# Query and key rows placed by head, so that one SBUF-to-SBUF transfer per block replaces the trip through DRAM

## The chip, the cores and the metric

The kernel runs on one NeuronCore of a Trainium2 chip. The metric is the device time of one launch in microseconds (us). Before the change three timed runs gave 1001.59 us in the median (996.12, 1001.59 and 1002.09); the execution that the profiler recorded took 993.12 us.

## What is computed

Two layers follow each other. The first is a linear attention with a complex decay, for 4 sequences of 768 steps with 8 heads of width 48:

```
mag = sqrt(a_re^2 + a_im^2);  a = (a_re, a_im) * min(mag, 0.999) / (mag + 1e-6)
for t in range(768):                       # for every batch and head
    S_re, S_im = a_re*S_re - a_im*S_im + outer(k[t], v[t]),  a_re*S_im + a_im*S_re
    y[t] = q[t] @ S_re                     # S: 48 x 48
```

The second is a mixture of four experts on the 3072 rows y (8 heads * 48 = 384 wide), with `p = domain_probs / (sum + 1e-9)`:

```
out = sum_e p[:, e] * (relu(x @ w1[e]) @ w2[e])      # w1: 384 x 1024, w2: 1024 x 384
```

All is float32. The matrix products of the experts are made from operands split into a high and a low part (names ending in h and l, three products for one).

## The kernel before, in words

**Groups.** The 3072 time steps are cut into 12 groups of 256 (g = 0 to 11), each of two chunks of 128 (c = 0, 1). A group's attention needs no step loop: with the running product A of the decays, the scores between q*A and k/A within a chunk are a matrix product, and a state Gs of [48 real + 48 imaginary rows, 8 heads, 48] carries what came before.

**Stage one** (0 to about 616 us) works as a pipeline. While TensorE runs the first two experts on group g-1 (`moe1`: eight steps, each of a first-layer part, tile `ph`, line 235, and a second-layer part, `po`, line 256), VectorE and ScalarE prepare group g (`norm`, `prefix`, `finish`: `head` makes Q, line 504, `tail` makes K, line 527). The attention of g is placed between the steps of group g-1 by `between`: from step `FIRST[g]` on (6, 5, 5, 4, 4 for groups 2 to 6, then 3) one piece of `attention` is issued per step. `advance` deals out the preparation by a budget of microseconds per step (`STEP`, `MORE`); `yield None` in `front` is a hold that lasts until the attention of g-1 has been issued. The framework then orders each engine's instructions by a simulated timeline, within the order that `behind` and `keep_in_program_order` fix; on the chip each engine runs its list in order.

**Rows.** Q and K are made with 128 of the 384 rows (head, component) on the partitions, in three columns j: row h*48+d lies at partition (h*48+d) mod 128. Heads 2 and 5 straddle two columns. The scores want each head's 48 components on partitions 0 to 47 (real) and 64 to 111 (imaginary): tiles `Qst` and `Kst`. For groups 2 to 11 `trip` (line 532) brings them there through DRAM: two transfers (real, imaginary) `q_d<-Q` or `k_d<-K` out (line 536) and two `Qst<-q_d` or `Kst<-k_d` back (line 543), all on SyncE's queue (SP). For groups 0 and 1 K goes by two TensorE transposes (lines 576 and 585, with ScalarE copies at 577 and 586) and Q by `pick` (matmuls with parts of the identity, group 0, chunk 0) or by `trip`.

**Attention of one group.** Before: the pieces are `turn0` (K of chunk 0 transposed into `KT`), scores of chunk 1 then chunk 0 (`sc`, line 619; VectorE multiplies them by a mask into `scs`, line 630); then `turn1`; then the values (`yp`, lines 650 and 660) of chunk 0 with the state increment of chunk 0 (`dp`, line 595; VectorE adds it to the state, line 605) inside them, behind the first pair of heads; then increment and values of chunk 1. The PSUM tiles of all of these share four buffers (tag "pa"). At the end `store_y` sends y to DRAM, `load_x` fetches it back as `xa`, and the next `moe1` starts on it.

**Behind it.** The loads of group g+1's inputs (`load_qk`, line 356, and `load_a`, line 349) wait until K of g has landed (`last["q"]`). `late_weights` (lines 780 to 802) runs beside the last groups: it loads weights (`lw`, line 784), sums and splits them on VectorE and ScalarE, and writes them to DRAM. **Stage two** (about 616 us to the end) runs the other two experts, lines 972 to 984, and touches nothing of the above.

Of the kernel before, what the change touches and what calls it, by code (L numbers as in the profile page):

```python
# [8 lines left out]
F32 = mybir.dt.float32  # L9
F32R = mybir.dt.float32r  # L10
AF = mybir.ActivationFunctionType
# [4 lines left out]
B, H, S, D = 4, 8, 768, 48  # L16
HD = H * D
# [43 lines left out]
STEP = {1: 4.2, 2: 4.2, 3: 4.2, 4: 4.2, 5: 4.2}  # L61
MORE = (1.5, 2.3, 0.5)
HOFF = 96
WIDE = 32 + P + 48
DMA_SCRATCH = 4096
XOF = (0, 1, 2, 3, 4, 5, 6, 7, 0, 8, 9, 6, 10, 11, 12, 13, 14, 15, 5, 9)
# [55 lines left out]
def fast_path(ctx, tc, qkP, aP, vP, probsP, w, out, flag):  # L122
# [164 lines left out]
    with ExitStack() as c1:  # L287
# [166 lines left out]
        def pick(g, nm, X, dst, s, w):  # L454
            n = 4 if w == C else 3
            for h0 in range(0, H, n):
                hs = range(h0, min(h0 + n, H))
                ps = ps_a.tile([M, len(hs), w], F32, tag="pa", name=f"{nm}p{g}_{s}_{h0}")
                for h in hs:
                    js = [j for j in range(NJ) if -D < h * D - j * P < P]  # L460
                    for j in js:
                        o = 32 + h * D - j * P
                        for c in range(2):
                            ins = nc.tensor.matmul(ps[c * IM:(IM, M)[c], h - h0, :], wide[:, o:o + (IM, D)[c]],
                                             X[:, c, j * CG + s, :w], start=(j == js[0]), stop=(j == js[-1]))
                nc.scalar.activation(dst[:, h0:h0 + len(hs), s, :w], ps, AF.Copy)
            return ins

# [60 lines left out]

            return Q, K, head, tail  # L530

        def trip(nm, X, dst, lo=0, hi=CG, prev=None):
            w = X.shape[-1] if hi == CG else C
            dt = dram.tile([2, HD, hi - lo, w], F32, name=nm)
            for c in range(2):
                sent = nc.sync.dma_start(dt[c].rearrange("(j p) n t -> p j n t", p=P),
                                         X[:, c].rearrange("p (j n) t -> p j n t", n=CG)[:, :, lo:hi, :w])
                if prev is not None:
                    behind(sent, prev)

            def back(prev=None):
                for c in range(2):
                    landed = nc.sync.dma_start(dst[c * IM:c * IM + D, :, lo:hi, :w],
                                               dt[c].rearrange("(h d) n t -> d h n t", d=D))
                    if prev is not None:
                        behind(landed, prev)
                return landed
            back.sent = sent
            return back

        def t_factors(g):
            Tr, Ti = Qst[0:D, :, CG - 1, C:], Qst[IM:M, :, CG - 1, C:]
# [9 lines left out]
        def chunk(g, c, K, y):  # L562
# [7 lines left out]
            def turned():  # L570
                if last and g >= NSEL:
                    return
                for i in range(2):
                    kt_ps = ps_a.tile([P, HD], F32, tag="pa", name=f"ktp{g}_{c}_{i}")
                    for j in range(NJ):
                        ins = nc.tensor.transpose(kt_ps[:, j * P:(j + 1) * P], K[0][:, i, j * CG + c, :], ident)
                    state["kt", g, c] = nc.scalar.activation(KT[:, c, :, i * IM:i * IM + D],
                                                             kt_ps.rearrange("p (h d) -> p h d", d=D), AF.Copy)
                return ins

            def turned_back():
# [57 lines left out]
                            behind(ins, prev)  # L639
                    nc.vector.tensor_tensor(scs[2 * c + hf], s_ps, near_mask.unsqueeze(1).broadcast_to([P, 4, C]), op=ALU.mult)  # L640

            def values(joined=False, after=None):
                y_ps = ps_a.tile([P, HP, C], F32, tag="pa", name=f"yp{g}_{c}")
                for p in reversed(range(HP)):
                    ws = (IM, D) if g < XSEL else (D, D)
                    pair = [(h * D, ws[u], y_ps[u * IM:u * IM + ws[u], p, :]) for u, h in enumerate((2 * p, 2 * p + 1))]
                    for o, n, yo in pair:
                        h = o // D
                        vo = o if h < HP else o + HD // 2
                        ins = nc.tensor.matmul(yo, vc[:, vo:vo + n], scs[2 * c + h // 4][:, h % 4, :],  # L650
                                               start=True, stop=first)
                        if joined:
                            tc.keep_in_program_order(ins)
                        if after is not None and p == HP - 1 and o == h * D and not h & 1:
                            behind(ins, wts["w1e"])
                        joined = True
                    if not first:
                        for o, n, yo in pair:
                            st = state[g, c].rearrange("m h d -> m (h d)")
                            ins = nc.tensor.matmul(yo, st[:, o:o + n], Qc[:, o // D, :], start=False, stop=True)  # L660
                            tc.keep_in_program_order(ins)
                    if after is not None and p == HP - 1:
                        after()
                state["yl", g, c] = ins
                for us in ((slice(0, M),) if g < XSEL else (slice(0, D), slice(IM, M))):
                    state["y", g, c] = nc.scalar.activation(y[us, :, cs], y_ps[us], AF.Copy)
# [30 lines left out]
        def near_attention(g, QK):  # L697
            Q, K = QK
            y = small.tile([M, HP, G], F32, tag="y", name=f"y{g}", bufs=1)
            (turn0, back0, inc0, sc0, val0), (turn1, back1, inc1, sc1, val1) = (chunk(g, c, K, y) for c in range(CG))  # L700
            if g == 0:
                state["pq"] = pick(g, "q", Q, Qst, 0, C)
                yield
            else:
                yield trip(f"q_d{g}_0", Q, Qst, 0, 1)()
                yield trip(f"q_d{g}_1", Q, Qst, 1)()
            state["tk"] = turn0()
            state["bk"] = back0()
            inc0()
            sc0((0,))  # L710
            if g > 0:
                sc0((1,))
            yield
            if g == 0:
                yield trip(f"q_d{g}", Q, Qst, 1)()
# [12 lines left out]
            rotate(g)  # L728
# [6 lines left out]
        def attention(g, QK):  # L735
# [2 lines left out]
            turn0()  # L738
            sc1()
            sc0(joined=True)  # L740
            yield turn1()
            val0(True, after=lambda: inc0(True))
            inc1(True)
            val1(True)
            t_factors(g)
# [71 lines left out]
        def front(g, A, qk):  # L817
# [34 lines left out]
            yield 3.9  # L852
            last["act"] = head(0, CG)
            yield 3.0
            qb = trip(f"q_d{g}", Q, Qst)
            yield None
            last["dve"] = tail(0, CG)
            yield 4.8
            kb = trip(f"k_d{g}", K[0], Kst)
            qb()  # L860
            last["q"] = kb()
            todo[g] = attention(g, (Q, K))

        x = {}
# [651 lines left out]
```

## Time and profile before

| What | Value |
|---|---|
| timed runs, median (lowest, highest) | 1001.59 us (996.12, 1002.09) |
| the profiled execution | 993.12 us, of which the span of instructions is 991.4 us |
| TensorE matmul busy | 936.7 us, 94% of the span |
| VectorE busy | 745.9 us, 75% |
| ScalarE busy | 479.4 us, 48% |
| GpSimd busy | 166.5 us, 17% |
| mean granted TensorE clock | 0.986 of full speed |
| DMA | 141.89 MB, HBM read 92.13 MB and written 48.43 MB |

Read the shares with the stages in mind: VectorE's 75% is 38 to 39 us in each cycle of some 41 to 48 us in stage one, and less in stage two. TensorE's full clock (1.0) is 2.4 GHz, 0.5 is 1.2 GHz.

### The profile page before, as it was taken

The numbers are of one execution on the slowest core, as the hardware profiler recorded it, in microseconds if no ns is written. First come the engines' busy times: TensorE is split into PE (matmuls) and PEld (weight loads), VectorE is DVE, ScalarE is ACT, GpSimd is POOL, SyncE is SP. The second block draws the span as 40 slices with busy tenths as digits, with TensorE's granted clock in tenths as the row PEclk, the third lists the DMA queues.
The fourth block names the chain that finished last, engine by engine and source line by source line (L and its number), as shares of the span: only waits on it lengthen the run. The fifth ranks groups of instructions, "written<-read, shape, count | busy, mean of one in ns | idle before, by whom it ended". The sixth has DMA issues, their size and how long they took to land.

```text
span 991.4 us, 18889 instructions
## 1 busy us (share of the span) xinstructions
PE 936.7 (94%) x7365; PEld 913.2 (92%) x7365; DVE 745.9 (75%) x1630; ACT 479.4 (48%) x954; POOL 166.5 (17%) x207
## 2 busy tenths in 40 slices
PE   5799989899999989989998999999999999999997
PEld 3699988898999989989998999999999999999997
DVE  7789979788989989969896583767676748576643
ACT  6756435263644727354453354645454546454430
POOL 6020000000000000000000005533433342323000
PEclk9899989999999999999999999999999999999999
DMA  9495274655748567484939769431513443231112
GB/s 317 121 200 154 64 193 109 169 132 154 170 149 189 155 146 185 107 198 129 222 110 262 274 191 305 101 97 48 129 48 116 158 137 101 66 97 48 49 48 75
DMA packets 99154, 141.89 MB, mean 143 GB/s; under 512 B 7360, under 2 KB 79728, under 8 KB 99056
## 3 DMA queue, kind: packets, MB, share of 16 engines
q1 hardware_dynamic: 87856, 113.80, 39.9%
q0 software_dynamic: 11200, 26.79, 11.6%
q8 instruction: 60, 0.98, 0.4%
q14 instruction: 38, 0.31, 0.1%
HBM read 92.13 MB, written 48.43 MB: 142 GB/s over the span
## 4 chain that ended last, share of the span: by engine, by line
PE 65%; DVE 13%; DMA 12%; ACT 6%; issue 2%; SPq 1%; DVEq 0%; ACTq 0%
PE pob L972 19%; PE pb L972 16%; PE ph L235 11%; PE po L256 10%; DMA Kst<-k_d 3%; PE sc L619 3%; DMA k_d<-K 2%; DMA q_d<-Q 1%; DMA lw<-w 1%; DMA wst<-w 1%; PE dp L595 1%; DVE scs L630 1%; PE yp L650 1%; PE yp L660 1%; DMA xa<-y_d 1%
## 5 line engine op out<-in xcount | busy, mean ns | idle before, releaser
L972 PE MATMUL pob<-shi,hid 128*128 128x384 f32 x528 | 148.6, 335 | 0.5 <-DVE hid L981 0.5
L256 PE MATMUL po<-whi,hh 128*128 128x384 f32 x384 | 131.6, 343 | 8.5 <-ACT acc L755 6.0
L256 PE MATMUL po<-wlo,hh 128*128 128x384 f32 x384 | 130.1, 339 | 0.0
L246 ACT ACTIVATE hh<-ph 128x512 fp32r<-128x512 f32 x96 | 56.8, 593 | 113.5 <-PE ph L235 113.0
L984 POOL TENSOR_TENSOR Z<-Z 128x384 f32<-128x384 f32 x84 | 89.7, 1088 | 109.1 <-DVE xl L978 46.2
L235 PE MATMUL ph<-xha,whi 128*128 128x256 f32 x576 | 103.3, 286 | 3.9 <-ACT xha L222 3.9
L235 PE MATMUL ph<-xla,whi 128*128 128x256 f32 x576 | 102.0, 285 | 1.3 <-DVE xla L224 1.3
L235 PE MATMUL ph<-xha,wlo 128*128 128x256 f32 x576 | 101.7, 283 | 0.0
L972 PE MATMUL pb<-xh,shi 128*128 128x384 f32 x291 | 97.2, 335 | 1.2 <-DVE pb L978 1.2
L972 PEld LDWEIGHTS pob<-shi,hid 128*128 128x128 f32 x528 | 96.5, 188 | 1.2 <-DVE hid L981 1.1
L972 PE MATMUL pb<-xl,shi 128*128 128x384 f32 x288 | 96.2, 334 | 0.0
L972 PE MATMUL pb<-xh,slo 128*128 128x384 f32 x288 | 96.2, 334 | 0.0
L235 PEld LDWEIGHTS ph<-xha,whi 128*128 128x128 f32 x576 | 86.7, 191 | 6.3 <-ACT xha L222 4.7
L972 PE MATMUL pob<-slo,hid 128*128 128x384 f32 x264 | 88.2, 334 | 0.0
L247 DVE SCALAR_TENSOR_TENSOR hl<-ph,hh 128x512 fp32r<-128x512 f32 x96 | 65.9, 687 | 28.9 <-ACT hh L246 28.1
L256 PE MATMUL po<-whi,hl 128*128 128x384 f32 x384 | 85.2, 339 | 1.6 <-DVE hl L247 1.5
L235 PEld LDWEIGHTS ph<-xla,whi 128*128 128x128 f32 x576 | 83.3, 191 | 2.3 <-DVE xla L224 1.5
L235 PEld LDWEIGHTS ph<-xha,wlo 128*128 128x128 f32 x576 | 83.0, 190 | 0.7 <-issue 0.7
L256 PEld LDWEIGHTS po<-whi,hh 128*128 128x128 f32 x384 | 73.2, 191 | 9.5 <-ACT acc L755 6.4
L975 ACT ACTIVATE SN<-pb 128x384 f32<-128x384 f32 x96 | 47.3, 492 | 67.0 <-PE pb L972 59.7
L978 DVE TENSOR_TENSOR xl<-Z,xh 128x384 fp32r<-128x384 f32 x104 | 60.1, 607 | 21.6 <-ACT xh L975 13.8
L256 PEld LDWEIGHTS po<-wlo,hh 128*128 128x128 f32 x384 | 73.3, 191 | 0.0
(233 smaller groups left out, 2039.7 us busy)
## 6 DMA issues: line engine op xcount, KB each, us to landing
qk<-qkP SPq DMA_DIRECT2D x24, 384.0 KB, 4.0
acc_d<-acc POOLq DMA_DIRECT2D x24, 384.0 KB, 4.9
ACC<-acc_d SPq DMA_DIRECT2D x48, 192.0 KB, 2.9
A<-aP SPq DMA_DIRECT2D x22, 384.0 KB, 5.8
q_d<-Q SPq DMA_DIRECT2D x20, 387.0 KB, 4.0
Qst<-q_d SPq DMA_DIRECT2D x20, 387.0 KB, 5.1
k_d<-K SPq DMA_DIRECT2D x20, 384.0 KB, 4.3
Kst<-k_d SPq DMA_DIRECT2D x20, 384.0 KB, 6.0
```

What stands on the lines that cost most here:

```text
L235: ins = nc.tensor.matmul(ph[:, u, :], wt[:, j * P:(j + 1) * P], xt[:, j, :], start=(n == 0), stop=(n == 3 * NJ - 1))
L246: wts["hh"] = nc.scalar.activation(hh, ph, AF.Relu)
L247: nc.vector.scalar_tensor_tensor(hl, ph, 0.0, hh, op0=ALU.max, op1=ALU.subtract)
L256: nc.tensor.matmul(po[t], part[0][:, u, t * P:(t + 1) * P], wts[i][n][:, HD:], start=(i % FE == 0 and part[0] is hh and n == 0), stop=(i % ...
L595: ins = nc.tensor.matmul(d_ps[o:o + n, h, :], KT[:, c, h, o:o + n], vc[:, h * D:(h + 1) * D], start=True, stop=True)
L619: ins = nc.tensor.matmul(to, k, q, start=True, stop=True)
L630: nc.vector.tensor_tensor(to, x, m.broadcast_to([m.shape[0], 4] + list(m.shape[2:])), op=ALU.mult)
L650: ins = nc.tensor.matmul(yo, vc[:, vo:vo + n], scs[2 * c + h // 4][:, h % 4, :], start=True, stop=first)
L972: return tc.keep_in_program_order(nc.tensor.matmul(*args, **kw))
L975: return pin(nc.scalar.activation(dst, src, fn, scale=scale))
L978: pin(nc.vector.tensor_tensor(dst, x, y, op=op))
L984: nc.gpsimd.tensor_tensor(dst, x, y, op=op)
```

## The change

The host lays the 384 rows out in another order, given by `ROWS` (first partition, count, columns, first component, first head): blocks of partitions, each of which holds for every column j one head's (or part of one head's) consecutive components. Partitions 0 to 47 hold heads 0, 1, 2 (columns 0, 1, 2), partitions 48 to 95 heads 3, 4, 5; the last 32 partitions hold heads 6 and 7: components 0 to 31 in columns 0 and 1, components 32 to 47 of both in column 2. With that each block goes from Q or K straight to its place in `Qst` or `Kst` by one transfer, `send`: five blocks times real and imaginary, ten transfers for Q and ten for K. `pick` and the copy of the transposed K (`turned`) follow the new order; the latter takes three ScalarE copies for one. The send of Q stands behind the hold and ahead of `tail`. In `attention` the first increment `inc0` moves from inside the values of chunk 0 to right behind the scores of chunk 0.

```diff
+ROWS = ((0, 48, (0, 1, 2), 0, 0), (48, 48, (0, 1, 2), 0, 3), (96, 32, (0, 1), 0, 6), (96, 16, (2,), 32, 6),
+        (112, 16, (2,), 32, 7))
...
-        def trip(nm, X, dst, lo=0, hi=CG, prev=None):
+        def send(X, dst, lo=0, hi=CG, prev=None):
             w = X.shape[-1] if hi == CG else C
-            dt = dram.tile([2, HD, hi - lo, w], F32, name=nm)
             for c in range(2):
-                sent = nc.sync.dma_start(dt[c].rearrange("(j p) n t -> p j n t", p=P),
-                                         X[:, c].rearrange("p (j n) t -> p j n t", n=CG)[:, :, lo:hi, :w])
-                if prev is not None:
-                    behind(sent, prev)
-            def back(prev=None):
-                for c in range(2):
-                    landed = nc.sync.dma_start(dst[c * IM:c * IM + D, :, lo:hi, :w],
-                                               dt[c].rearrange("(h d) n t -> d h n t", d=D))
+                src = X[:, c].rearrange("p (j n) t -> p j n t", n=CG)[:, :, lo:hi, :w]
+                for p, n, j, d, h in ROWS:
+                    landed = nc.sync.dma_start(dst[c * IM + d:c * IM + d + n, h:h + len(j), lo:hi, :w],
+                                               src[p:p + n, j[0]:j[-1] + 1])
                     if prev is not None:
                         behind(landed, prev)
-                return landed
-            back.sent = sent
-            return back
+            return landed
...
-                    state["kt", g, c] = nc.scalar.activation(KT[:, c, :, i * IM:i * IM + D],
-                                                             kt_ps.rearrange("p (h d) -> p h d", d=D), AF.Copy)
+                    kj, to = kt_ps.rearrange("t (j p) -> t j p", j=NJ), KT[:, c, :, i * IM:i * IM + D]
+                    nc.scalar.activation(to[:, :6].rearrange("t (a j) d -> t a j d", j=NJ),
+                                         kj[:, :, :2 * D].rearrange("t j (a d) -> t a j d", d=D), AF.Copy)
+                    nc.scalar.activation(to[:, 6:, :32], kj[:, :2, 2 * D:], AF.Copy)
+                    state["kt", g, c] = nc.scalar.activation(
+                        to[:, 6:, 32:], kj[:, 2, 2 * D:].rearrange("t (h d) -> t h d", d=16), AF.Copy)
...
             turn0()
             sc1()
             sc0(joined=True)
+            inc0(True)
             yield turn1()
-            val0(True, after=lambda: inc0(True))
+            val0(True, begin=True)
             inc1(True)
             val1(True)
...
-            qb = trip(f"q_d{g}", Q, Qst)
             yield None
+            send(Q, Qst)
             last["dve"] = tail(0, CG)
             yield 4.8
-            kb = trip(f"k_d{g}", K[0], Kst)
-            qb()
-            last["q"] = kb()
+            last["q"] = send(K[0], Kst)
```

In `near_attention` (groups 0 and 1) each `trip(...)()` becomes a `send`. In `pick` a head of the last block takes two matmuls per part, each of its own rows, where heads 2 and 5 took two that added up; the count stays. `tiled` on the host indexes the rows of q, k and a by the new order.

## Rows read from the trace of the kernel before

**Rows 1.** The list of waits of TensorE over the run: who waited, for what, us in total, times, longest.

```profile
PE sc L619 <- DMA Kst<-k_d: 9.3, 4, 3.2
PE sc L619 <- issue: 2.8, 1, 2.8
```

**Rows 2.** The timeline of TensorE, the score matmuls of groups 2, 3, 4, 5 and 7: start, us, instruction, count, and in brackets the idle time before them.

```profile
141.38 5.39 PE L619 MATMUL sc<-Qst,Kst 112*64 112x128 f32 x64 [3.19 <-DMA Kst<-k_d]
184.92 4.43 PE L619 MATMUL sc<-Qst,Kst 112*64 112x128 f32 x64 [2.85 <-DMA Kst<-k_d]
231.25 4.27 PE L619 MATMUL sc<-Qst,Kst 112*64 112x128 f32 x64 [2.25 <-DMA Kst<-k_d]
275.62 2.91 PE L619 MATMUL sc<-Qst,Kst 112*64 112x128 f32 x64 [1.00 <-DMA Kst<-k_d]
360.00 2.92 PE L619 MATMUL sc<-Qst,Kst 112*64 112x128 f32 x64 [2.79 <-issue]
```

**Rows 3.** The chain of waits: the trip of K of group 2, out and back (the second of each pair), and the trips out of groups 3, 4, 5 (second) and 7 (first): start, us, what.

```profile
129.17 5.92 DMA k_d<-K
135.11 6.13 DMA Kst<-k_d
...
174.84 3.75 DMA k_d<-K
...
222.44 2.81 DMA k_d<-K
...
264.97 6.10 DMA k_d<-K
...
348.01 2.88 DMA k_d<-K
```

**Rows 4.** TensorE in short stretches: length, busy us (count), granted clock, share of the DMA engines, GB/s. The first three are the stretches at half clock behind the waits of groups 2, 3 and 4, the last is the scores of group 5.

```profile
140.37:147.20 6.83, 5.82 (x66) 0.50 0.66 222
184.74:188.16 3.42, 3.24 (x41) 0.50 0.70 219
232.53:235.94 3.41, 3.41 (x42) 0.50 0.99 330
275.60:278.60 3.00, 2.98 (x65) 1.00 0.68 211
```

**Rows 5.** Issue and landing of transfers on SP: two issues in a row in the timeline; the profile's list of issues (KB each, median us from issue to landing); and, from the answer on line 543, duration of an issue (ns, min/median/max) and its time to landing.

```profile
141.26 0.83 SPq L356 DMA_DIRECT2D qk<-qkP  x2
...
qk<-qkP SPq DMA_DIRECT2D x24, 384.0 KB, 4.0
...
y_d<-y SPq DMA_DIRECT2D x24, 192.0 KB, 3.1
...
L543 SPq DMA_DIRECT2D Kst<-k_d x20: 320/321/1982, 134.1 to 533.2; - x20
...
DMA to landing us min/median/max: 2.9/5.1/10.4
```

**Rows 6.** All engines from K of group 2 to K of group 7 (length; PE, PEld, DVE, ACT, POOL busy; clock; DMA; GB/s), and VectorE's wait for the scores from 55 to 616 us.

```profile
129.17:348.88 219.71, 205.97 (x1998) 200.43 (x1998) 188.94 (x421) 103.78 (x192) 5.72 (x8) 0.97 0.61 156
...
DVE scs L630 <- PE sc L619: 14.0, 8, 4.2
```

**Rows 7.** ScalarE's copy of the transposed K, and the smallest copies that it makes (busy us, mean ns, idle before); and the second transposes of group 1, chunk 1, which wait for it.

```profile
L577 ACT ACTIVATE KT<-ktp 128x384 f32<-128x384 f32 x40 | 18.1, 487 | 43.7 <-PE ktp L576 43.6
L553 ACT ACTIVATE TA<-Qst 48x8 f32<-48x8 f32 x12 | 2.6, 213 | 0.2
...
95.58 1.08 PE L585 MATMUL kp<-wide,KT 128*112 128x128 f32 x8 [0.64 <-ACT KT L577]
```

**Rows 8.** What the moved increment meets: VectorE's masking of the scores of chunk 1 in group 5 and of the scores in group 11, TensorE's scores of group 11, and TensorE's wait for the state at line 660.

```profile
277.19 1.08 DVE L630 TENSOR_TENSOR scs<-sc,maskp 128x256 f32<-128x256 f32 x3 [1.25 <-PE sc L619]
...
278.63 0.43 DVE L630 TENSOR_TENSOR scs<-sc,maskp 64x256 f32<-64x256 f32 x1
...
551.43 1.51 DVE L630 TENSOR_TENSOR scs<-sc,maskp 128x256 f32<-128x256 f32 x4
...
547.11 2.91 PE L619 MATMUL sc<-Qst,Kst 112*64 112x128 f32 x64
...
L660 PE MATMUL yp<-Qst,Gs 112*48 112x128 f32 x320 | 33.8, 273 | 0.9 <-DVE Gs L605 0.9
```

**Rows 9.** The timeline around K of group 11: SP's issues, VectorE's and ScalarE's waits beside them, and TensorE's wait.

```profile
527.03 1.47 SPq L536 DMA_DIRECT2D k_d<-K  x2
528.55 3.62 SPq L784 DMA_DIRECT2D lw<-w  x4
...
532.80 0.97 DVE L798 TENSOR_TENSOR lwm<-lw,lwt 128x256 fp32r<-128x256 f32 x3 [3.40 <-DMA k_d<-K]
...
535.38 0.62 ACT L797 ACTIVATE lwt<-lw 128x256 fp32r<-128x256 f32 x2 [7.41 <-DMA lw<-w]
...
539.04 0.44 PE L256 MATMUL po<-whi,hh 128*128 128x384 f32 x1 [4.57 <-ACT acc L755]
```

**Rows 10.** ScalarE's wait for the trip of Q, 55 to 616 us; and, in the timeline of group 0, SP's issue of Q of chunk 1 and GpSimd's copy that waits for its landing (the weight casts stand behind it).

```profile
ACT u L408 <- DMA q_d<-Q: 9.2, 7, 2.8
...
38.23 0.91 SPq L536 DMA_DIRECT2D q_d<-Q  x2
...
44.70 0.17 POOL L874 COPY tick<-Qst 1x1 f32<-1x1 f32 x1 [28.23 <-DMA Qst<-q_d]
```

More of the change, by code (lines that the diff above doesn't have):

```diff
@@ L459, in pick @@
                 for h in hs:
-                    js = [j for j in range(NJ) if -D < h * D - j * P < P]
-                    for j in js:
-                        o = 32 + h * D - j * P
+                    for p, n, j, d, hp in ROWS:
+                        if not hp <= h < hp + len(j):
+                            continue
                         for c in range(2):
-                            ins = nc.tensor.matmul(ps[c * IM:(IM, M)[c], h - h0, :], wide[:, o:o + (IM, D)[c]],
-                                             X[:, c, j * CG + s, :w], start=(j == js[0]), stop=(j == js[-1]))
+                            m = n + (IM - D if c == 0 and d + n == D else 0)
+                            ins = nc.tensor.matmul(ps[c * IM + d:c * IM + d + m, h - h0, :], wide[:, 32 + p:32 + p + m],
+                                                   X[:, c, j[h - hp] * CG + s, :w], start=True, stop=True)
                 nc.scalar.activation(dst[:, h0:h0 + len(hs), s, :w], ps, AF.Copy)
@@ L640, in near_scores, with values @@
                     nc.vector.tensor_tensor(scs[2 * c + hf], s_ps, near_mask.unsqueeze(1).broadcast_to([P, 4, C]), op=ALU.mult)
-            def values(joined=False, after=None):
+            def values(joined=False, begin=False):
                 y_ps = ps_a.tile([P, HP, C], F32, tag="pa", name=f"yp{g}_{c}")
@@ L653, in values @@
                             tc.keep_in_program_order(ins)
-                        if after is not None and p == HP - 1 and o == h * D and not h & 1:
+                        if begin:
                             behind(ins, wts["w1e"])
-                        joined = True
+                        joined, begin = True, False
                     if not first:
@@ L661, in values @@
                             tc.keep_in_program_order(ins)
-                    if after is not None and p == HP - 1:
-                        after()
                 state["yl", g, c] = ins
@@ L704, in near_attention @@
             else:
-                yield trip(f"q_d{g}_0", Q, Qst, 0, 1)()
-                yield trip(f"q_d{g}_1", Q, Qst, 1)()
+                yield send(Q, Qst, 0, 1)
+                yield send(Q, Qst, 1)
             state["tk"] = turn0()
@@ L714, in near_attention @@
             if g == 0:
-                yield trip(f"q_d{g}", Q, Qst, 1)()
+                yield send(Q, Qst, 1)
             tk = turn1()
@@ L1480, in rows @@
         return x.transpose(0, 1, 3, 2).reshape(B, HD, S)
+    place = np.zeros((NJ, P), dtype=np.int64)
+    for p, n, j, d, h in ROWS:
+        for i in range(len(j)):
+            place[j[i], p:p + n] = (h + i) * D + d + np.arange(n)
     def tiled(x):
-        x = x.reshape(2, B, NJ, P, GB, CG, CS, SEG).transpose(1, 4, 3, 0, 7, 2, 5, 6)
+        x = x[:, :, place.reshape(-1)].reshape(2, B, NJ, P, GB, CG, CS, SEG).transpose(1, 4, 3, 0, 7, 2, 5, 6)
         return np.ascontiguousarray(x).reshape(NG, P, 2 * NJ * G)
```

## Prediction

> **What bounds the kernel now.** I read the shares of the page first: TensorE is busy 94% of the span, so only its idle time and its slow time can be won. The list of TensorE's waits names them. The scores wait for the transfers of K in five groups, 9.3 us in four of them and 2.8 us in a fifth [rows 1]; that one is put down to "issue", but it starts where the first of two K transfers landed and ends where the second did. The timeline shows the waits one by one: 3.19, 2.85, 2.25, 1.00 and 2.79 us in groups 2, 3, 4, 5 and 7, together 12.1 us [rows 2]. The chain of waits shows what runs meanwhile: in group 2, K leaves at 129.17 us, is in DRAM 5.92 us later, and the way back takes another 6.13 us [rows 3], 12.1 us in all. Last I read the granted clock. Behind the waits of groups 2, 3 and 4 it fell from full speed (2.4 GHz) to half (1.2 GHz) for 6.83, 3.42 and 3.41 us [rows 4], and the same 64 score matmuls took 5.39, 4.43 and 4.27 us there against 2.91 us in group 5 at full speed [rows 2].
>
> **The trip of K becomes one transfer.** The change removes four transfers (two out, two back) for each of Q and K, and adds ten. Issue first: two issues in a row took 0.83 us on SP, 0.415 us each [rows 5]. Ten then start over 9 x 0.415 = 3.7 us. Landing: no row shows SBUF to SBUF, and none fewer than 48 partitions. The nearest is y to DRAM, also from 48 partitions in runs of 1 KB: 3.1 us [rows 5]. The best case is nothing added over the pitch; the worst is the slowest K landing, 10.4 us [rows 5]. I take 3.1, the row nearest in shape. The send of K takes 3.7 + 3.1 = 6.8 us from its first issue. The second component's trip began 0.9 us after the first, so that is 5.9 to 6.0 us from the point at which the trip took 12.1 us; 6 us are won.
>
> TensorE came to the scores, that is, start less wait [rows 2], 9.0, 7.2, 6.6 and 9.7 us after the second K issue in groups 2 to 5, and 9.2 us after the first in group 7 [rows 3]. The send needs 6.0 (or 6.8) there, so all five waits go: -12.1 us. With them goes the half clock. By matmuls alone it cost (5.39 - 2.91) + (4.43 - 2.91) + (4.27 - 2.91) = 5.4 us [rows 2]; if everything in the 13.7 us at half speed scales, 6.8 us [rows 4]. I take 6.0. Gain **18.1 us**; its other end is the first rival.
>
> **What stands behind the longer issue.** SP now issues 20 transfers a group (8.3 us) instead of 8. Behind the K send stand the input loads of the next group, which waited for K to land anyway and now come sooner. Between y's store and `xa` up to ten Q issues may stand, 4.2 us; the store's landing (3.1 us) covers three quarters of that, and if that cover is gone a group's first step starts some 1 us late. I cost it at nothing, since the trip's own transfers leave the queue too. In group 0 the send of Q of chunk 1 ends 6.8 us after its start at 38.23, at 45.0, and the GpSimd copy, with the weight casts behind it, started at 44.70 [rows 10]: 0.3 us on work that TensorE needs only in later steps, nothing.
>
> Q's source buffer is held longer: ScalarE waited 9.2 us in seven groups for Q's first transfer [rows 10], and the send lands 1 to 2 us later than that. VectorE's `norm` hangs on it. I charge 1.5 us in total; it is nothing where TensorE paces, 7 x 2 = 14 us where it does not.
>
> **ScalarE's three copies for one.** The copy takes 487 ns, a tiny one 213 ns [rows 7]; two more add at most 0.43 us, less a little for the shorter first. In groups 2 to 11 `KT` is needed by `dp` some us later, so nothing shows. In groups 0 and 1 transposes, copies and second transposes follow each other, and TensorE did wait 0.64 us for `KT` [rows 7]. Two copies stand in the way per chunk, 0.7 us; chunk 0 has other matmuls beside it, chunk 1 of both groups has not: **+1.4 us**, between 0 and 2.8.
>
> **The increment beside the scores.** The same matmuls run earlier, but they need a fifth PSUM tile of "pa", which has four buffers: two for each chunk's scores. So `dp` waits until VectorE has masked one tile of chunk 1. In group 5 three of the four operations end at 278.27 and the fourth at 279.06, while TensorE ends the scores at 275.62 + 2.91 = 278.53 [rows 2, 8]: a wait of -0.3 to +0.5 us, I take 0.1 in each of nine groups, +0.9. In group 11 the scores end at 550.02 and the masking at 552.94 [rows 8]: up to 2.9 us; I take half, +1.5, as that order comes from weight sums whose input landed late. The state's wait of 0.9 us at line 660 goes [rows 8]. Together **+1.5 us**.
>
> **The last group.** K of group 11 is issued at 527.03, behind it four loads of `lw`; VectorE waited 3.40 us for K's first transfer to free the buffer, ScalarE 7.41 us for `lw`, and TensorE stood 4.57 us [rows 9]. Eight more issues ahead of `lw` are 3.3 us; less traffic gives some back, and the loads might be put ahead. **+2.5 us**, between 0 and 5.
>
> **The sum:** -18.1 + 1.5 + 1.4 + 1.5 + 2.5 = -11.2 us of the profiled 993.12 us, -1.13%. The median of the runs shown, 1001.59, is 0.9% above the profiled execution; the same share of it gives **990 us**.
>
> The Trainium skill, "DMA: Bandwidth & Descriptors", section "Rules for kernel authors", speaks against the change: small transfers should be joined into one, since below 64 KB a transfer is mostly overhead (the smallest block here is 16 partitions of 1 KB). With that page's fixed 2 us paid ten times in a row a send would be an estimated 20 us. The trace agrees with the overhead but not with paying it in a row: transfers issued 0.415 us apart land in 4.0 us each [rows 5]. A send by that rule would be rival 2 below at a still slower pitch, and of its chance I give the rule 0.02.
>
> **Rival 1, VectorE paces the early groups.** From K of group 2 to that of group 7 VectorE was busy 188.9 of 219.7 us, TensorE 206.0 [rows 6]. If VectorE's list cannot run tighter, the next K is not made sooner, TensorE meets a new wait at the next scores, and only the first wait with its half clock is won: 3.2 + 3.4 = 6.6 us, less the 6.9 us of costs: about **1002 us**. For it: the two engines stand within 17 us of each other. Against it: VectorE itself waited 14.0 us for those scores [rows 6], time that comes back with the waits, and the send's 6 us are a further reserve.
>
> **Rival 2, the blocks issue slowly.** Some issues took 1.98 us instead of 0.32 [rows 5]. The trip's length is met at a pitch of (12.1 + 0.9 - 3.1) / 9 = 1.1 us; from there the change loses. At 1.5 us a send takes 16.6 us from its first issue, K lands 3.6 us later than now: 5 x 3.6 = 18 us on top of the waits there are, none won, with 6.9 of costs about **1027 us**. Against it: the median issue is 0.32 us and a block has fewer rows than what is issued now.
>
> **Rival 3, the increment holds TensorE.** If VectorE is late everywhere as in group 11, ten waits of 2.9 us, 29 us instead of 2.4, turn -11.2 into +15: **1017 us**. It decides from a mean wait of 1.4 us, where it eats the gain. Against it: group 5's 0.5 us at most.
>
> **How the numbers follow.** Within 1% (10 us) is about what a measurement of this kernel can't tell from no change, so 991.6 and 1011.6 are the bounds. Chances: the forecast 0.62, rival 1 0.22, rival 2 0.08, rival 3 0.08. The forecast's own range is 979 (the costs vanish) to 998 (half the gain is lost): seven tenths of it lie below 991.6, so faster 0.43; same takes its rest, 0.18, and rival 1, 0.22, 0.40 in all; slower is rivals 2 and 3 and a little of rival 1, 0.17. The range of 8 in 10 runs from 978 to 1007: it takes in the forecast and rival 1.
>
> **What would show it.** The waits of the scores for K should be gone or under 0.5 us each, the clock should hold full speed through groups 2 to 7, and the last K transfer of a group should land 6 to 7 us after VectorE's first K. SP's block issues should stand 0.4 us apart. `dp` should begin within 0.5 us of the scores' end, with a longer idle in group 11 alone; `lw` should be issued some 3 us later behind K of group 11. The prediction is wrong if waits of 2 us or more at the scores come back in groups 3 to 7 with VectorE busy throughout (rival 1), if sends take 12 us or more (rival 2), or if TensorE stands ahead of `dp` in every group (rival 3). New orders of whole engines' lists, which a profile of before can't show, would be a fourth cause.

## The result and the profile after

The kernel after took 971.0 us (970.5 to 971.8) beside 999.5 us (996.1 to 1002.1) of the kernel before: ratio 0.972, interval 0.968 to 0.975. Faster, below the range of 978 to 1007, with 2.5 times the forecast gain. Beside later runs of the kernel before (about 993 us) it took 969.5 us, ratio 0.9755, interval 0.971 to 0.980 (e12). The two profiled executions, on which the sums below rest, stand 22.5 us apart (993.12 and 970.57 us; spans 991.4 and 968.9).

The page after: span, TensorE's busy time, its granted clock in 40 slices, and the shares of the chain that ended last.

```profile
span 968.9 us, 19262 instructions
...
PE 934.6 (96%) x7365; PEld 905.6 (93%) x7365; DVE 745.2 (77%) x1630; ACT 484.4 (50%) x1034; POOL 167.9 (17%) x207
...
PEclk9899999999999999999999999999999999999999
...
PE 83%; DVE 6%; ACT 5%; DMA 3%; issue 1%; SPq 1%; ACTq 0%; DVEq 0%
```

Span less TensorE's busy time is its idle time: 991.4 - 936.7 = 54.7 us before, 968.9 - 934.6 = 34.3 us after. So 20.4 of the 22.5 us are waits that went, and 2.1 us are matmuls that ran faster. In the chain DMA fell from 12% to 3%.

TensorE's waits after, from 55 to 620 us (who, for what: us in total, times, longest):

```profile
PE po L258 <- ACT hh L248: 1.7, 2, 0.9
PE po L258 <- DVE hl L249: 1.6, 2, 1.4
PE po L258 <- ACT acc L753: 1.6, 2, 1.1
PE ph L237 <- DVE xla L226: 1.4, 1, 1.4
PE ph L237 <- ACT xha L224: 1.2, 2, 0.6
...
PE kp L584 <- ACT KT L573: 0.7, 1, 0.7
```

No far score waits for K any more: the 12.1 us of [rows 1] are gone. The kernel before had in the same stretch also 6.0 us of `po` for `acc` (one of 4.57, [rows 9]) and 3.3 us of `ph` for `xha` (one of 2.7):

```profile
PE po L256 <- ACT acc L755: 6.0, 2, 4.6
PE ph L235 <- ACT xha L222: 3.3, 2, 2.7
```

These fell by 4.4 and 2.1 us, and the 0.9 us for the state [rows 8] went. Half clock stood behind both longest ones too, 3.41 us each in blocks 8 and 10, so that before it came to 20.5 us after the start and not to the 13.7 us of [rows 4]:

```profile
437.33:440.74 3.41, 3.41 (x14) 0.50 0.98 183
539.73:543.14 3.41, 3.41 (x14) 0.50 1.10 234
```

The scores of groups 2, 5 and 7 after, answering to [rows 2] (start, us, instruction, count; no idle time ahead):

```profile
138.43 0.43 PE L618 MATMUL sc<-Qst,Kst 112*64 112x128 f32 x2
139.70 2.58 PE L618 MATMUL sc<-Qst,Kst 112*64 112x128 f32 x55
...
263.15 2.91 PE L618 MATMUL sc<-Qst,Kst 112*64 112x128 f32 x64
...
346.17 2.91 PE L618 MATMUL sc<-Qst,Kst 112*64 112x128 f32 x64
```

In group 2 other matmuls stand between the first scores and the rest: the list of TensorE is a new one. From K of group 2 to K of group 7 (length; PE, PEld, DVE, ACT, POOL busy; clock; DMA; GB/s), answering to [rows 6], and the only stretch at half clock, at the start, in which TensorE still had work:

```profile
129.38:335.79 206.41, 203.32 (x1989) 194.52 (x1989) 188.94 (x421) 105.90 (x223) 5.72 (x8) 1.00 0.46 126
28.54:35.36 6.82, 3.73 (x36) 3.33 (x40) 4.77 (x15) 4.03 (x10) 0.00 (x0) 0.50 0.01 3
```

219.7 us became 206.4, with VectorE as busy as before. The blocks behind it, to the end of the span, gave another 10 us (643.4 to 633.1 us), and K of group 2 starts 1.1 us later.

The send of K in group 2, its ten issues and SP's next work in the timeline; then, over the run, the duration of an issue of K (ns, min/median/max) and the time to landing of all sends, Q and K:

```profile
129.38 6.25 SPq L540 DMA_DIRECT2D Kst<-K  x10
...
136.94 0.83 SPq L358 DMA_DIRECT2D qk<-qkP  x2
```

```profile
L540 SPq DMA_DIRECT2D Kst<-K x100: 514/590/1716, 129.4 to 518.5; - x100
...
DMA to landing us min/median/max: 1.7/3.1/5.6
```

The last block lands at 136.93 us, 7.55 us after the first issue. Before, K of group 2 landed 12.94 us after its first issue.

### The profile page after: what moved, and what is told of

The parts are those of the page before. It is cut to its first block, busy times and chain, and to the rows that moved or that the text cites. A ratio compares the mean times of both kernels' runs of the same rounds, so it can differ in the third digit from the quotient of the medians.

```text
span 968.9 us, 19262 instructions
## 1 busy us (share of the span) xinstructions
PE 934.6 (96%) x7365; PEld 905.6 (93%) x7365; DVE 745.2 (77%) x1630; ACT 484.4 (50%) x1034; POOL 167.9 (17%) x207
## 4 chain that ended last, share of the span: by engine, by line
PE 83%; DVE 6%; ACT 5%; DMA 3%; issue 1%; SPq 1%; ACTq 0%; DVEq 0%
PE pob L968 20%; PE ph L237 18%; PE po L258 18%; PE pb L968 16%; PE sc L618 3%; PE yp L649 2%; PE dp L594 2%; PE yp L659 1%; DMA wst<-w 1%; PE ktp L571 1%; DVE scs L629 1%; SPq L540 1%; PE xp L688 1%; DVE xl L974 1%; ACT y L663 0%
## 5 line engine op out<-in xcount | busy, mean ns | idle before, releaser
L974 DVE TENSOR_TENSOR xl<-Z,xh 128x384 fp32r<-128x384 f32 x104 | 60.0, 607 | 21.6 <-ACT xh L971 11.4
L971 ACT ACTIVATE hid<-pb 128x384 fp32r<-128x384 f32 x76 | 37.3, 490 | 72.3 <-PE pb L968 71.9
```

Of the source, the lines that this page charges most:

```text
L971: return pin(nc.scalar.activation(dst, src, fn, scale=scale))
L974: pin(nc.vector.tensor_tensor(dst, x, y, op=op))
```

## The experiments

Each edit is against the kernel after or before, as named; the ratio is to the kernel before on the same chip. Lines of the scores are L618 to L629 by kernel.

**e1: the increment back among the values** (kernel after).

```diff
-            inc0(True)
             yield turn1()
-            val0(True, begin=True)
+            val0(True, after=lambda: inc0(True))
```

> The changed kernel with one part undone: the first increment goes back inside the values of chunk 0; rows and sends stay. Theory T (the sends alone make the gain, because K lands 5 to 6 us sooner and TensorE neither waits nor loses its clock): 968 to 975 us, no wait of the scores for K, no stretch at half clock after 40 us. Rival I (the moved increment carries part of it, as it takes 32 matmuls off the values and reorders TensorE's list): 978 us or more, new waits at lines of the values or of the state.

967.4 us, ratio 0.973 (0.969 to 0.978): the whole gain without the moved increment.

**e2: the moved increment alone** (kernel before, the same lines the other way round).

> The kernel before with the moved increment alone; Q and K still go through DRAM. Theory T: within 1% of before (990 to 1005 us), the scores wait for K in four to six groups with 9 to 14 us in total and the clock falls behind them as before. Rival I: 975 to 988 us. My prediction's own price for the increment (it holds TensorE behind VectorE) would give 1.5 us more than before and waits at the increment's first matmul.

988.9 us, 0.995 (0.993 to 0.998). The waits for K stayed, and grew:

```profile
PE sc L619 <- DMA Kst<-k_d: 13.8, 5, 3.8
...
PE po L256 <- ACT acc L754: 1.6, 2, 1.1
PE ph L235 <- ACT xha L222: 1.2, 2, 0.6
```

Yet it is a little faster: what fell are the late waits, for `acc` (6.0 before) and for `xha` (3.3 before).

**e3: every block cut by head** (kernel after; 20 transfers for a send, not the 16 that the text on record counts).

```diff
-                    landed = nc.sync.dma_start(dst[c * IM + d:c * IM + d + n, h:h + len(j), lo:hi, :w],
-                                               src[p:p + n, j[0]:j[-1] + 1])
...
+                    for i in range(len(j)):
+                        landed = nc.sync.dma_start(dst[c * IM + d:c * IM + d + n, h + i, lo:hi, :w], src[p:p + n, j[i]])
```

> The changed kernel with each block's transfer cut by head: 16 transfers for Q and 16 for K instead of 10, same bytes, no DRAM. At the changed kernel's measured pitch of 0.63 us an issue a send then lasts 15 x 0.63 + 1.9 = 11.4 us from its first issue instead of 7.6, nearly as long as the trip (12.9). Theory T (only the landing time of K counts): K lands 3.8 us later, waits of the scores for K come back in groups 2 to 5 with 3 to 12 us in total, and with them stretches at half clock: 975 to 990 us. Rival D (the gain comes from 17 MB less of DRAM traffic, whatever the landing time): 969 to 973 us, as changed. If an issue with fewer rows is cheaper than 0.63 us (0.35), a send is as long as in the changed kernel and both give 971.

1011.1 us, 1.016 (1.011 to 1.022). An issue costs the same (590 ns at the median) for as little as a third of the bytes, so a send lasts twice as long: in group 3 SP issued for 14.17 us. TensorE waits not at the scores but for x of the next block (and 4.1 us once for `acc`):

```profile
PE ph L237 <- ACT xha L224: 13.8, 6, 6.1
```

**e4: the kernel before once more.**

> The kernel before, unchanged, profiled a second time: how much its waits for K vary. The first profile took 993.1 us while its timed runs took 996 to 1002. Theory T: the timed runs have longer waits for the trip than the profiled one had, so this profile, if it is near 1000 us, shows more than 12 us of waits of the scores for K and more half clock. Rival V (the extra 6 us lie elsewhere, at the start or in stage two): same 12 us of waits at the scores, and stage one as long as in the first profile.

991.0 us, 0.999 (0.997 to 1.001), with its waits for K.

**e5 and e6: one tensor through DRAM again** (kernel after, groups 2 to 11): Q in e5, K in e6. `trip` sends two transfers out and brings the ten blocks back, in the new order of rows.

```diff
+        def trip(nm, X, dst):
+            w = X.shape[-1]
+            dt = dram.tile([2, P, NJ, CG, w], F32, name=nm)
+            for c in range(2):
+                nc.sync.dma_start(dt[c], X[:, c].rearrange("p (j n) t -> p j n t", n=CG))
+            for c in range(2):
+                for p, n, j, d, h in ROWS:
+                    landed = nc.sync.dma_start(dst[c * IM + d:c * IM + d + n, h:h + len(j), :, :w],
+                                               dt[c, p:p + n, j[0]:j[-1] + 1])
+            return landed
...
-            send(Q, Qst)
+            trip(f"q_d{g}", Q, Qst)
```

> The changed kernel, but Q goes through DRAM again (two transfers out, ten back into the blocks' places); K keeps its send. Theory T (what counts is when K lands): K's send stands behind Q's way back on SP and starts 1 to 4 us later, still ahead of the trip of before; few or no waits of the scores for K: ratio to before 0.972 to 0.985. Rival D (half the gain belongs to Q, through traffic or queue): ratio 0.985 or more with no waits at the scores.

> The changed kernel, but K goes through DRAM again (two out, ten back); Q keeps its send. The way of K is then 4.5 us out, ten issues of 0.63 us and 3 us to land, some 14 us against 12.9 before. Theory T: the waits of the scores for K come back in groups 2 to 7, 10 to 25 us with their half clock, ratio 0.985 to 1.01. Rival D: 0.98 or less.

970.7 us, 0.976 (0.973 to 0.979), and 975.7 us, 0.981 (0.977 to 0.984). In e6 K needs 9 to 11 us from its first issue in five of groups 2 to 7, and the scores of these groups wait 0.6 us in all. That only K's landing time counts can't be the whole story.

**e7 and e8: the late waits of the kernel before.** e7 puts Q's way out behind the hold; e8 orders the copies to `lwt` behind the `acc` copies of block 10. The edit of e7:

```diff
-            qb = trip(f"q_d{g}", Q, Qst)
             yield None
+            qb = trip(f"q_d{g}", Q, Qst)
```

> The kernel before with Q's trip out moved behind the hold, as the change has it for the send; all else as before. In before's profile SP issued Q's way out of group 9 ahead of y's store of group 8, which blocked for 2.2 us, and TensorE waited 2.7 us for xa with 3.4 us at half clock behind it. Theory H (the place of Q's transfer behind the hold takes that wait away): no xa wait at block 8, 3 to 5 us less, ratio 0.994 to 0.998. Rival: the wait stays, ratio 0.998 to 1.003; or Q then delays K's trip and the waits for K grow, ratio above 1.003.

> The kernel before with one order fixed: ScalarE's copies of the second late weights come behind the accumulator copies of block 10's first expert, as they do in the changed kernel's list. In before's profile TensorE waited 4.6 us for those accumulator copies, which stood on ScalarE behind copies that waited 7.4 us for a load, and ran 3.4 us at half clock after it. Theory A (that order alone cost 5 to 6 us): wait gone, ratio 0.993 to 0.996. Rival (the load comes late for VectorE too, and the wait moves to hl or to the scores of group 11): ratio 0.998 to 1.002.

992.5 us, 0.999 (0.997 to 1.001), and 992.9 us, 1.000 (0.998 to 1.002). Neither is the cause: in e7 both waits stay, in e8 the wait for `acc` moves to `hl` (4.9 us in total beside 1.5).

**e9: both tensors through DRAM**, e5 and e6 together; **e12: the kernel after** beside it.

> The kernel after with Q and K both through DRAM again, in the new order of rows: per tensor two transfers out and ten back, the next group's Q or K queued behind them. Theory D (direct transfers are what counts): with either tensor direct the other's trip was cheap, with both through DRAM nothing is left of the gain; K lands 8 us or more after its first issue, the scores wait 2 us or more in at least three of groups 2 to 7, ratio 0.995 or above. Theory P (place in TensorE's list is what counts: K arrives in ten pieces, the planner then puts expert matmuls ahead of the scores): K lands as late, 8 to 13 us after its first issue, but the scores' waits are under 1 us each in groups 2 to 7, and the ratio is 0.975 to 0.988.

> The kernel after once more, beside the three others on the same chip. Both theories: 0.970 to 0.976. It is the mark against which the parts are read: what e11 reaches of its gain came by place alone, what lies between the two needs the direct transfers or the moved increment.

971.2 us, 0.977 (0.972 to 0.982), and 969.5 us, 0.9755 (0.971 to 0.980). With no direct transfer in groups 2 to 11 the gain is the same; DMA moves 140.7 MB, nearly as before (141.9; the kernel after 124.9). TensorE's waits in e9 from 55 to 620 us, the three that are over a microsecond; none is for K:

```profile
PE ph L237 <- ACT xha L224: 3.2, 3, 2.0
PE po L258 <- ACT acc L764: 3.1, 3, 1.5
PE ph L237 <- DVE xla L226: 1.7, 1, 1.7
```

**e10: the way back of K cut into pairs of heads** (kernel before, eight transfers for two). **e13: the same for Q and K, with the moved increment.** The edit of e10:

```diff
-                    landed = nc.sync.dma_start(dst[c * IM:c * IM + D, :, lo:hi, :w],
-                                               dt[c].rearrange("(h d) n t -> d h n t", d=D))
...
+                    for h0 in range(0, H, 2 if nm[0] == "k" else H):
+                        hs = slice(h0, h0 + (2 if nm[0] == "k" else H))
+                        landed = nc.sync.dma_start(dst[c * IM:c * IM + D, hs, lo:hi, :w],
+                                                   dt[c].rearrange("(h d) n t -> d h n t", d=D)[:, hs])
```

> The kernel before; only the way back of K from DRAM is cut into four transfers of two heads for each component (eight for two). Rows, Q's trip and the increment stay as before. Theory P (pieces change the list): the written-out list has other matmuls ahead of or between the scores in groups 2, 3, 4 and 8 only, so the waits of the scores go in those and stay at 1 us or more in groups 5 and 7; ratio 0.983 to 0.992. Theory D (direct transfers): six more issues on SP make K later by up to 2.5 us, waits stay or grow in groups 2 to 5 and 7, ratio 0.998 to 1.01.

> The kernel before, with its rows and its trips through DRAM, changed in two things: the way back of Q and of K in groups 0 and 2 to 11 is cut into transfers of two heads (eight for two), and the increment stands beside the scores as in the kernel after. Theory C (cutting into pieces, with the list of TensorE that follows from it, and the moved increment make the gain; rows and direct transfers add nothing): e10's 1.3% and e2's 0.5% add up, ratio 0.978 to 0.985. Theory R (the new order of rows, which makes the way out one run per partition and the trip 2 us shorter, carries a part of its own): little more than e10, ratio 0.985 to 0.990, K waits of 1 us and more left in groups 2 and 7.

981.2 us, 0.987 (0.982 to 0.992), and 974.2 us, 0.982 (0.979 to 0.984). Cut into pieces the old trip gives half of the gain, and with the increment three quarters. In e10 the waits for K fell from 12.1 to 3.1 us, those for `xha` grew from 3.3:

```profile
PE ph L235 <- ACT xha L222: 6.5, 6, 3.2
PE sc L621 <- DMA Kst<-k_d: 2.9, 3, 1.4
```

**e14: e9 with the heads of the far scores in falling order**, so that the first score needs the last block of K.

```diff
-                for h in range(4):
-                    for u, f in ((0, 0), (1, 0), (1, 1), (0, 1)):
+                for h in reversed(range(4)):
+                    for u, f in ((1, 0), (0, 0), (0, 1), (1, 1)):
```

> e9 (both tensors through DRAM in ten pieces back), with the heads of the far scores taken in falling order, so that the first of them needs the last block of K to land. Theory S (scores gain by starting on the blocks that have landed): the first score is later by up to 2 us in groups 2 to 5 and 7, waits of 1 to 3 us are back in them, ratio 0.983 to 0.993. Theory L (the place in the list is what counts): the written-out list has 2 to 9 more expert matmuls ahead of these scores, no wait over 0.5 us in these groups, ratio 0.975 to 0.981.

970.9 us, 0.980 (0.976 to 0.984), no wait for K: a start on blocks that have landed is not what the cut gives. TensorE comes to the scores of groups 2 to 5 and 7 10.4 to 11.7 us after K's first issue, where before it came after 7.4 to 10.5 us and stood waiting.

**e15: e9 with the increment back among the values** (e1's edit).

> e9 with the increment back among the values, so that of the change only the new rows stay, with the cut into pieces that they bring and the split of ScalarE's copy. Theory C: the increment's part is the 0.3 to 0.5% of e2 at most, ratio 0.976 to 0.983; a theory that the increment is what let the late waits go (for x and acc in blocks 8 and 10): they come back with their half clock, 10 us more, ratio 0.986 to 0.992.

982.3 us, 0.989 (0.987 to 0.992). The waits for K are gone here too, but two others come to 11.5 us, where e9 had 3.2 us for `xha` and none for `hh`:

```profile
PE po L258 <- ACT hh L248: 5.8, 4, 3.2
PE ph L237 <- ACT xha L224: 5.7, 3, 3.8
```

The trace shows where. Group 4 in e15, the group with the largest difference: K's first issue, the first scores, the store of y, the load of `xa`, and the wait of the next block:

```profile
211.20 1.12 SPq L550 DMA_DIRECT2D k_d<-K  x2
...
222.29 1.57 PE L629 MATMUL sc<-Qst,Kst 112*64 112x128 f32 x32
...
243.90 0.95 SPq L743 DMA_DIRECT2D y_d<-y  x2
248.43 0.38 SPq L217 DMA_DIRECT2D xa<-y_d  x1
...
252.91 0.73 PE L237 MATMUL ph<-xha,whi 128*128 128x256 f32 x3 [3.81 <-ACT xha L224]
```

The same in e9, where that wait does not occur:

```profile
214.79 1.02 SPq L550 DMA_DIRECT2D k_d<-K  x2
...
225.79 1.57 PE L629 MATMUL sc<-Qst,Kst 112*64 112x128 f32 x32
...
240.75 1.38 SPq L741 DMA_DIRECT2D y_d<-y  x2
244.60 0.38 SPq L217 DMA_DIRECT2D xa<-y_d  x1
```

From K to the scores both take 11 us. From the scores to y's store e15 takes 21.6 us, e9 15.0. What the moved increment does is to bring y, and with it x of the next block, sooner. Not in every group: e1 and the kernel after differ by 0.2 us in group 4. But in groups 5 and 8 it does so in all five pairs with the increment in either place (before and e2, e1 and after, e10 and e13, in which Q's trip differs too, e15 and e9, e16 and e17). In group 8 y's store begins 18.9 to 20.1 us after the first scores with the increment among the values, 12.9 to 13.5 us with it beside the scores; in the other groups some pairs show no difference or, in group 10, 1.7 us the other way. Scores and store of group 8, first before, then e2, in which no wait for `xha` follows:

```profile
403.94 2.91 PE L619 MATMUL sc<-Qst,Kst 112*64 112x128 f32 x64
...
423.93 1.09 SPq L733 DMA_DIRECT2D y_d<-y  x2
```

```profile
406.04 2.91 PE L619 MATMUL sc<-Qst,Kst 112*64 112x128 f32 x64
...
418.95 0.94 SPq L731 DMA_DIRECT2D y_d<-y  x2
```

**e16: the first far score ordered behind a later expert matmul**, in groups 2 to 5 and 7 of the kernel before, where `mo.flush()` also issues the waiting second-layer part ahead of the attention; trips and the rest unchanged; **e17: the same with the moved increment; e11: the attention of these groups a whole step of a block later.**

```diff
+LATE = {2: 0, 3: 7, 4: 7, 5: 3, 7: 7}
...
-                            behind(ins, wts["w1e"])
+                            behind(ins, wts["w2"][LATE[g]] if g in LATE else wts["w1e"])
...
+                    if g in LATE and k == first:
+                        mo.flush()
                     r = next(todo[g], None)
```

```diff
-FIRST = {1: 5, 2: 6, 3: 5, 4: 5, 5: 4, 6: 4}
+FIRST = {1: 5, 2: 7, 3: 6, 4: 6, 5: 5, 6: 4, 7: 4}
```

> The kernel before; only the step of a block at which the next group's attention is started is one later for groups 2, 3, 4, 5 and 7, so that about one step (12 to 30 expert matmuls) more stands ahead of the scores. All transfers as before. Theory P (place in the list): K's trip takes its 12 us as before, yet the scores' waits in groups 2 to 5 and 7 fall under 0.5 us each, with the half clock behind them; 12 to 18 us less, ratio 0.982 to 0.990. Theory D (K's arrival paces the kernel, a later place only moves the wait): TensorE waits as long elsewhere, for x of the next group or for the values, and the ratio is 0.997 to 1.01.

> The kernel before with its rows, trips and increment; only the first far score of groups 2, 3, 4, 5 and 7 is ordered behind a later expert matmul at line 256 (the 1st, 8th, 8th, 4th and 8th of the next twelve), so that TensorE comes to the scores some 1 to 4 us later than before and not a whole step later, as in e11. Theory P (the place in the list, the same trip): waits for K under 0.7 us in at least three of the five groups, 5 to 12 us less, ratio 0.987 to 0.995. Rival (K has to come sooner, a later place only hands the wait on to x of the next group): waits for K or for xha of 2 us and more stay in three of the groups or more, ratio 0.997 to 1.006.

> e16 with the increment beside the scores as in the kernel after; rows and trips as before, nothing cut into pieces. Theory P: e16's part and the moved increment's 0.5 to 1.1% add up, ratio 0.978 to 0.988. Rival: 0.993 to 1.002, e2's half per cent at best, since the shorter trip of pieces or of direct transfers is what the rest of the gain needs.

e11: 1002.3 us, 1.010 (1.007 to 1.012). e16: 1002.5 us, 1.013 (1.010 to 1.016). e17: 980.7 us, 0.990 (0.987 to 0.993). First e16, then e17:

```profile
PE ph L236 <- ACT xha L223: 12.7, 7, 3.5
PE po L258 <- ACT acc L757: 6.4, 3, 4.4
PE sc L621 <- DMA Kst<-k_d: 3.1, 1, 3.1
```

```profile
PE sc L621 <- DMA Kst<-k_d: 6.4, 2, 3.3
PE ph L236 <- ACT xha L223: 3.1, 3, 1.9
```

In both, the waits for K in groups 3, 4, 5 and 7 are gone with the trip of before, so the place in the list does take them away. (In e11 they are gone in groups 4, 5 and 7; 9.0 us are left in groups 2, 3 and 11.) But in e16, as in e11 (15.5 us for `xha`), TensorE then waits for x of the next block instead: theory P was right on K and wrong on the time. Yet e16 is not the small delay of 1 to 4 us that was wanted. Its first K issue and first scores of group 5:

```profile
257.56 1.23 SPq L538 DMA_DIRECT2D k_d<-K  x2
...
280.78 2.46 PE L621 MATMUL sc<-Qst,Kst 112*64 112x128 f32 x52
```

That is 23.2 us, beside 10.5 before and 24.2 in e11; in group 4 it is 16.4 beside 7.4. What a delay of 1 to 4 us with the increment among the values would give was not run. With the increment moved (e17) the later place costs nothing, and the ratio is half a per cent below e2's; the two intervals touch.

## Why the prediction was wrong

**The step that failed is the costs.** Of the profiled execution I forecast 11.2 us less, and 22.5 went. Of the 6.9 us that I set against the gain next to nothing is to be seen; the largest of them, 2.5 us more of TensorE's wait for `acc` in the last group, came out as 4.4 us less for `acc` in all. Waits that I had put at nothing went as well, 2.1 us for `xha` and 0.8 for `hh`. The half clock, a term of the gain, gave 3.9 us less than its 6.0. The terms in turn:

**The score waits went, as forecast** (12.1 us). The send has a pitch between issues of 0.63 us in groups 2 to 4 and 0.71 to 0.75 in groups 5 to 7, not 0.415 [rows 5], and lands in 3.1 us as estimated: 7.5 to 9.9 us from first issue to last landing in groups 2 to 7, 6.8 forecast. It sufficed, with some help from the new list: at the times after K's first issue at which TensorE came to the scores before, groups 4 and 7 would have waited 1.0 and 0.7 us for these sends. The Trainium skill's page "DMA: Bandwidth & Descriptors", section "Rules for kernel authors", would have had the small transfers joined. In their direction the runs agree (e3, twice as many transfers, 1.6% slower than before), but not in the estimate of 20 us for a send (the page gives its fixed 2 us for transfers that GpSimd issues): ten in a row took 7.55 us, nine pitches of 0.63 us and 1.9 us from the last issue to its landing.

**The half clock was over-counted.** I took 6.0 us for 13.7 us of it; all 20.5 us went, and TensorE's busy time fell by 2.1 us in all, the scores' line by 3.0 (34.5 to 31.5). The slow scores were slow as read, but part is given back: the line of `dp` rose by 0.9 us (22.3 to 23.2). Whether scores that now alternate with other matmuls cost the rest was not tried. As forecast, the clock is at full speed through groups 2 to 7.

**The costs of 6.9 us did not come.** ScalarE's three copies take 419 + 235 + 220 = 874 ns for 487, but TensorE's wait for `KT` only rose from 0.6 to 0.7 us (forecast 1.4 for the whole term). K of group 2 starts 1.1 us later, but in e7 and e8, with the one copy, it starts 1.1 and 1.4 us later too, so that this is no sign of the copies:

```profile
L573 ACT ACTIVATE KT<-ktp 128x288 f32<-128x288 f32 x40 | 16.8, 419 | 28.1 <-PE ktp L571 27.9
L575 ACT ACTIVATE KT<-ktp 128x64 f32<-128x64 f32 x40 | 9.4, 235 | 0.0
L576 ACT ACTIVATE KT<-ktp 128x32 f32<-128x32 f32 x40 | 8.8, 220 | 0.0
```

`dp` waits nowhere for a buffer (forecast 1.5 us), because 0.8 to 3.0 us of expert matmuls stand between the scores and `dp` in the new list; I had set it right behind them. ScalarE's waits of 9.2 us for Q's way out [rows 10], which I had grow by 1.5, are gone; ScalarE now waits once for Q's send, 5.6 us ahead of a late weight's split, and no wait of TensorE follows. The last group (2.5) came out the other way: `lw` waits behind K's ten issues as forecast, 7.87 us of SP from 511.25, but the new list has the `acc` copies ahead of `lwt`, and the 4.57 us of [rows 9] went instead of growing. I had built a cost on an order of ScalarE's list that the change replaced. That this order is the reason is not shown: alone it only moved the wait to `hl` (e8), and with the increment moved alone (e2) 0.4 us of the 4.57 was left.

**The rest I had not priced at all**: the waits for `xha` and `acc` in blocks 8 and 10, and with them the reason why the increment matters. I asked what the increment would hold up and not what it stood in front of. It sat inside the values of chunk 0, ahead of y, its store, `xa` and the next block's first matmuls. The runs point to this chain, K, scores, values, y, x, as what has to fit into a block:

| | increment among the values | increment beside the scores |
|---|---|---|
| trip of before | 1 | 0.995 (e2) |
| trip cut in pairs | 0.987 (e10) | 0.982 (e13) |
| trip in ten blocks, new rows | 0.989 (e15) | 0.977 (e9), 0.980 (e14) |
| direct send | 0.973 (e1) | 0.972, 0.9755 (after, e12) |
| scores later, trip of before | 1.013 (e16) | 0.990 (e17) |

The chain can be relieved at its head, with K landing 1.8 us sooner on the mean of groups 2 to 7 by a direct send (e1 beside e15, 1.6%), or in its middle, with the increment out of the way of y (e9 beside e15, 1.2%; e17 beside e16, 2.3%). With both there is more room than is needed: e1, e9 and the kernel after are equal within their intervals. So the change's two parts look like two cures for one shortage. With the increment moved, the words "not through DRAM" are not what the time hangs on; with it among the values, 1.6% hangs on them.

**And the scaling.** I put the sum, 981.9 us, up by 0.9% to 990, since the median shown was that much above the profiled execution. The kernel after has no such distance (970.57 profiled, 971.0 median): 8 of the 19 us of the miss are this step, 11 the sum. Rival 1 fell (VectorE was busy 188.9 of 206.4 us, and TensorE had no new wait), so did 2 and 3. The fourth cause that I named and did not price, new orders of whole lists, is the nearest to what happened.

**What stays open.** Why cutting the trip makes the scores' place later is seen in the traces, not explained by them: the order is made ahead of the run by the planner (the framework's simulated timeline), and no run changed its view of a transfer alone. Nor did one separate, in e9, the shorter trip (10.4 us on the mean of groups 2 to 7 beside 11.3) from the later place. That the waits for `acc` in block 10 belong to the same chain was argued from e2 and e17, where they are small, and not tried by itself; in e1, with the increment among the values and a direct send, there is none either.

## What to carry to other kernels

A wait names the last link; before pricing its removal, follow the chain on to where the next block needs its result, and ask what else stands in that chain: moving a later link (e17) can be worth as much as a faster transfer. Where a planner writes the engines' lists, a cost or a wait that rests on its present order is not a term to carry over; bound it from both sides, gains included. And test an obvious cause by putting the old path back with the rest kept: in e9, with both tensors through DRAM, the gain stayed. One such run is not enough, though: e15 shows that the direct send counts again once the increment stands where it was.

## What was not expected of the hardware

An issue of a block from SBUF to SBUF takes SP 590 ns at the median, 48 partitions by three heads or 16 by one alike (e3), beside 320 ns for a whole component from DRAM [rows 5] and 419 ns for the same ten blocks from DRAM (e9). Landing of a block is 3.1 us direct and 3.5 us from DRAM at the median, so what the direct path saves is mainly the way out. With one contiguous run per partition that way out is itself shorter, 2.9 us at the median to landing beside 3.9:

```profile
L550 SPq DMA_DIRECT2D k_d<-K x20: 320/338/574, 130.9 to 512.0; - x20
...
DMA to landing us min/median/max: 2.3/2.9/6.1
```
